# A two-layer transformer prompt kernel: the first tiles' statistics, the last output and the instruction order rearranged

## The chip, the core and the metric

The kernel runs on one core of a Trainium2 chip. The metric is the device time of one execution in microseconds. TensorE multiplies matrices (PE in the profile, PEld its weight loads), VectorE (DVE) and ScalarE (ACT) do elementwise work, GpSimd (POOL) a few masks at the start, and SyncE (SP) issues nearly all transfers between DRAM and on-chip memory. PSUM is the memory in eight banks into which TensorE accumulates.

## The reference

x is 2048 x 1024 in bf16. Two layers are computed with the same weights, each an attention part and a feed-forward part, both behind a layer norm and with a residual:

```
x = x + A(layernorm(x))      # qkv = x @ wqkv; 32 heads of 32; each position attends
                             # to 8 positions: itself and every second one before it; @ wo
x = x + B(layernorm(x))      # relu(x @ w1 + b1)**2 @ w2 + b2, inner width 3584
x = x + A(layernorm(x))
x = x + B(layernorm(x))
```

## The kernel before, in words

The 2048 rows are four blocks of 512 per layer, eight units u in all; a block is four tiles (tl) of 128 rows. A unit goes through: load and normalise x (SA), transpose it so that TensorE can contract over the width, the q, k and v products (SQ in eight-block form, SQ7 in a form with seven products of half blocks that needs sums and differences of weights), windowed attention (S2), the wo product and second layer norm (SW, SW7), and the two feed-forward products (SF1, SF2). The combined weights are made once in the first blocks and kept in DRAM tensors (sk, sqv, sw, two, tw); later blocks read them back. tw1 is one of the four combinations of w2, read in two halves by SF2.

Nothing is issued directly. Every step is an operation of a Plan with an engine, an assumed duration, a priority and the cells that it reads and writes. `Plan.schedule` plays the operations with these durations and takes on each engine the ready one with the lowest priority number; `emit` does so once per list in `ORDER`. The seeds of the first list move some priorities up or down by a hashed amount (`shift`), those of the later lists do so around the start times of the schedule before (`reshift`). The order thus found is the order in which the instructions stand on each engine; each engine executes its own in that order and waits by semaphores. SP too works through its transfers in that order, and a transfer also waits until the one that used the same of eight semaphores before it has landed. So new seeds move instructions everywhere.

The opening (SA for u = 0). Tiles are taken in the order `ORD` = 0, 1, 3, 2. `load_x` (the issue is recorded at L418, inside `dma`) loads a tile by SP, or by ScalarE for the tiles in `XACT`. Tiles 0 and 1 go through `ln_first`: two statistics of 512 columns on VectorE (L787), their aggregate (L789), logarithm and exponential on ScalarE (L780, L781), the normalisation on VectorE (L784), and then `transpose`: eight 128 x 128 transposes on TensorE (L803) into one PSUM bank and copies out of it (L806), in two parts of 512 columns. Tiles 2 and 3 (`LNA`) go through `ln`: sums and squares on ScalarE (L742, L746) and the normalisation on VectorE (L755, tile 3) or ScalarE (L721, tile 2), with one copy by ScalarE out of PSUM. `first` and `after` add dependencies: tile 1's statistics come after tile 0's last statistic, and tile 0's normalisation after tile 1's aggregate. Before all this TensorE runs 15 products of ones, and four more after tile 1's transposes (`keep_clock`, L1493). The first real products are those of q and k (SQ, L882), for the columns of tiles 0 and 1 first; their first chunk is in two parts, the first of which needs only the first part of the copies.

The transposes of later blocks are made by transfers (L768, `DMA_TRANSPOSE`) instead of TensorE.

The end (SF2 of the last unit, `out_tile`). The product T4 accumulates into the banks X[0] and X[1]. X[1] is the last, and its last seven contraction steps are split into two halves of 256 columns. `out_tile` with `end` adds each half of the bank to the residual xm on VectorE (L1450) and stores it; all other outputs go by a cast on ScalarE (L1051) and an addition on VectorE (L1052).

## Time and profile before

| | us |
|---|---|
| median of three runs | 1133.62 |
| lowest and highest | 1131.38, 1135.53 |
| the profiled execution | 1133.11 |
| its span in the profile | 1131.4 |
| TensorE busy | 1119.1 |
| VectorE busy | 991.6 |
| ScalarE busy | 814.4 |

The page counts an engine as busy while one of its instructions runs; matmuls overlap one another, and their ends are modelled. A row of the timeline merges equal neighbours: start, length from the first start to the last end, engine, line, operation, tiles, shape, count, and in brackets the idle time before with what ended it. A row of the issues gives the tensor, the queue, the count, the size of one transfer and the median time from issue to landing. A row of the waits gives who waited for whom: total, times, longest.

### The profile page before, as it was taken

Reading aid. Unit: us, or ns where it says so; the run is one execution under the profiler, and the core shown is the slowest. Engines: PE = TensorE matmul, PEld = TensorE weight load, DVE = VectorE, ACT = ScalarE, POOL = GpSimd, SP = SyncE. Lnnn points to the kernel's source line nnn. Section 1 sums busy time; section 2 is a strip of 40 time slices with the busy share of each in tenths; the row PEclk is TensorE's granted clock in tenths of the full one; section 3 lists DMA queues with packets and bytes.
Section 4 is the critical chain, followed back from the end, with each engine's and each line's share of the span. In section 5 each row is a group of like instructions: output and inputs, shape, how many; then the busy total and the mean of one; then the engine's idle time right before and its main releaser. Section 6 shows DMA issues by size and latency. Waiting matters only on the chain.

```text
span 1131.4 us, 20642 instructions
## 1 busy us (share of the span) xinstructions
PE 1119.1 (99%) x7856; PEld 770.6 (68%) x7903; DVE 991.6 (88%) x1527; ACT 814.4 (72%) x1631; POOL 1.8 (0%) x8
## 2 busy tenths in 40 slices
PE   9999999999999999999999999999999999999998
PEld 6645764678746887468864788557884678845864
DVE  6999999999996999969999699997999799996341
ACT  7747996568975799556994669937798378933961
POOL 0000000000000000000000000000000000000000
PEclk9999999999999999999999999999999999999999
DMA  9956899999899988999879997899969999589881
GB/s 369 288 190 204 269 326 327 337 356 375 345 362 361 330 358 310 297 392 330 355 288 346 399 365 271 296 381 364 395 212 351 374 363 388 197 297 341 340 302 62
DMA packets 137022, 362.35 MB, mean 320 GB/s; under 512 B 67418, under 2 KB 68570, under 8 KB 116570
## 3 DMA queue, kind: packets, MB, share of 16 engines
q1 hardware_dynamic: 136634, 360.50, 90.9%
q8 instruction: 62, 1.02, 0.4%
q10 hardware_dynamic: 288, 0.52, 0.1%
q14 instruction: 38, 0.31, 0.1%
HBM read 314.84 MB, written 31.46 MB: 306 GB/s over the span
## 4 chain that ended last, share of the span: by engine, by line
PE 92%; ACT 5%; DMA 2%; issue 1%; DVE 0%; ACTq 0%; DVEq 0%; SPq 0%
PE X L659 26%; PE X L1382 15%; PE Z L659 13%; PE Z L1382 7%; PE Y L659 7%; PE pq L882 6%; PE py L481 4%; PE Y L1382 4%; PE py L1078 4%; PE X L1149 3%; PE Z L1149 2%; PE lg L959 1%; DMA w<-in_B_w_dram 1%; PE Y L1149 1%; DMA xt<-xs 1%; ACT r L1317 1%
## 5 line engine op out<-in xcount | busy, mean ns | idle before, releaser
L659 PEld LDWEIGHTS <-w 128*128 128x128 bf16 (+1 forms) x4904 | 479.6, 98 | 71.3 <-DMA w<-sw 1.2
L1382 PEld LDWEIGHTS <-r 128*128 128x128 f16 x1183 | 115.7, 98 | 136.5 <-issue 1.7
L1382 PE MATMUL X<-w,r 128*128 128x512 f16 (+2 forms) x784 | 176.1, 377 | 1.6 <-ACT yxa L1051 1.3
L944 DVE TENSOR_TENSOR P<-q,k 128x2048 f16<-128x2048 f16 x128 | 154.3, 1221 | 2.4 <-ACT q L622 0.9
L659 PE MATMUL X<-T,w 128*128 128x256 f16 x1224 | 154.2, 273 | 0.3 <-ACT u L1286 0.3
L1023 DVE TENSOR_TENSOR pr<-pb,v 128x4096 f16<-128x4096 f16 x64 | 146.2, 2293 | 0.5
L952 DVE TENSOR_TENSOR P<-P,P 128x2048 f16<-128x2048 f16 x110 | 133.3, 1215 | 0.1
L1317 ACT ACTIVATE r<-rr 128x1024 f16<-128x1024 f16 x110 | 124.2, 1147 | 0.2
L1030 DVE TENSOR_TENSOR pr<-pr 128x2048 f16<-128x2048 f16 (+1 forms) x128 | 117.7, 947 | 0.0
L659 PE MATMUL X<-TA,w 128*128 128x256 f16 x864 | 107.2, 273 | 0.1
L882 PE MATMUL pq<-xnA,w 128*128 128x256 f16 (+1 forms) x512 | 86.1, 326 | 0.2 <-ACT k L887 0.2
L592 ACT COPY Y<-X 128x512 f32<-128x512 f32 x115 | 70.3, 611 | 19.8 <-PE X L659 15.3
L1296 ACT CAST y<-Z 128x512 f16<-128x512 f32 x110 | 70.3, 655 | 7.3 <-PE Z L659 7.1
L882 PEld LDWEIGHTS <-w 128*128 128x128 bf16 x512 | 49.9, 98 | 32.6 <-issue 0.7
L1300 DVE TENSOR_TENSOR rr<-u,y 128x512 f16<-128x512 f16 x110 | 45.5, 419 | 25.2 <-ACT y L1296 16.6
L1323 ACT ACTIVATE rr<-Y,b1T 128x256 f16<-128x256 f32 x110 | 54.6, 536 | 4.9 <-PE Y L659 4.3
L659 PE MATMUL X<-xnB,w 128*128 128x256 f16 x440 | 56.1, 273 | 0.1
L659 PE MATMUL Y<-xnB,w 128*128 128x256 f16 x440 | 56.0, 273 | 0.0
L614 ACT CAST yq<-Z 128x512 f16<-128x512 f32 x72 | 41.5, 586 | 19.7 <-PE Z L659 19.7
L1323 ACT ACTIVATE rr<-X,b1T 128x256 f16<-128x256 f32 x110 | 55.6, 570 | 0.0
L1051 ACT CAST yxo<-X 128x512 f16<-128x512 f32 x27 | 15.4, 586 | 55.5 <-PE X L1382 55.5
L610 ACT CAST u<-X 128x512 f16<-128x512 f32 x72 | 41.5, 586 | 18.6 <-PE X L659 18.1
(166 smaller groups left out, 1684.6 us busy)
## 6 DMA issues: line engine op xcount, KB each, us to landing
w<-sw SPq DMA_DIRECT2D x49, 1024.0 KB, 9.1
w<-tw SPq DMA_DIRECT2D x56, 896.0 KB, 6.7
w<-in_B_w_dram SPq DMA_DIRECT2D x42, 896.0 KB, 5.3
w<-in_B_w_dram SPq DMA_DIRECT2D x35, 1024.0 KB, 9.8
w<-in_A_wqkv_dram SPq DMA_DIRECT2D x32, 1024.0 KB, 10.1
w<-sqv SPq DMA_DIRECT2D x24, 1024.0 KB, 10.5
w<-in_B_w_dram SPq DMA_DIRECT2D x28, 512.0 KB, 6.3
w<-sk SPq DMA_DIRECT2D x12, 1024.0 KB, 8.2
```

The source lines that it names most:

```text
L592: self.p.add("ACT", act(512), lambda: self.nc.scalar.copy(Y[:], X[:]), [(X, 0)], [(Y, 0)], UP, name="u")
L659: nc.tensor.matmul(bank[:, a, :], lw[:, k, a * 128:(a + 1) * 128], rhs(k), start=(start and k == 0 and a == 0), stop=(k == 3), skip_group_ ...
L882: nc.tensor.matmul(pq[:, t0 * HB:t1 * HB], w[:, c0 // 2 % 2, kd // 4, kd % 4, c0 % 2 * 128:c0 % 2 * 128 + 128], xnT[:, 2 * t0:2 * t1, kd, ...
L944: nc.vector.tensor_tensor(cur[:], q[:, c, None, hb * HB:(hb + 1) * HB].to_broadcast([128, W, HB]), _win_ap(k[:, c, :], HALO + hb * HB, HB) ...
L952: nc.vector.tensor_tensor(other[:], other[:], cur[:], ALU.add)
L1023: p.add("DVE", dve(4096), lambda pr=pr, ch=ch: nc.vector.tensor_tensor(pr[:], pb[:].unsqueeze(1).to_broadcast([128, 2, W, HB]), _win_ap2(v ...
L1030: nc.vector.tensor_tensor(dst, pr[:, :, 0:n, :], pr[:, :, n:2 * n, :], ALU.add)
L1149: nc.tensor.matmul(bank[q][:], left(j, q), right(j), start=start and j == 0, stop=j == h - 1, skip_group_check=True)
L1296: p.add("ACT", act(512), lambda: nc.scalar.copy(y[:], bank[:]), [(bank, 0)], [(y, 0)], 1.5, name="y")
L1317: p.add("ACT", 0.955, lambda: nc.scalar.activation(out=r2[:, f:f + 2, :].rearrange("p a t -> p (a t)"), in_=r[:].rearrange("p a m t -> p ( ...
L1323: p.add("ACT", 0.36, lambda a=a: nc.scalar.activation(out=r[:, a, 0, :], in_=bank[:, a, :], func=ACTF.Relu, bias=self.b1T[:, f + a:f + a + ...
L1382: nc.tensor.matmul(banks[q][:, lo:hi], left(jj, q), w[:, j, lo:hi], start=(start and jj == 0), stop=(jj == h - 1), skip_group_check=True)
```

## The change

Opening: all four tiles of x are loaded by SP, in the order 0, 1, 3, 2 (`XACT` empty). Tile 3 leaves `LNA` and goes through `ln_first`, so its statistics and normalisation are VectorE's, and its copy too; only tile 2's statistics stay on ScalarE. Tile 1's statistics now come after tile 0's aggregate (`AGF`) instead of its last statistic, and tile 3's after tile 1's normalisation (`FNO`) instead of its copy. Where a tile's copies are in two parts, the second part goes to ScalarE (`CPA`).

End (`TAIL`): before the last, split contraction steps TensorE adds the residual of the last tile into its bank by one product with the identity. The bank is then copied out by two plain copies, the first half by VectorE with a store on SP's queue, the second by ScalarE with a store on ScalarE's queue.

Order: new seeds, in two lists instead of three.

```diff
-XACT = (1, 2)
+XACT = ()
...
-LNA = (2, 3)
+LNA = (2,)
+LNP = -9e4
+LNV = (3,)
+AGF = True
+FNO = True
+CPA = (1,)
+TAIL = True
...
 ORDER = [   # 55, 18 and 19 seeds replaced by 52 and 23 others
...
-            p.add("DVE", 0.5, f4, [(x, 0), (sm, 0), (sm, 1)], [(xn, 0)], -2e5 + pr, after=after, name="bn4")
-            return self.transpose(xn, xnT, tl, -1e5 + pr, 2 if tl < 2 else 1), xn
+            no = p.add("DVE", 0.5, f4, [(x, 0), (sm, 0), (sm, 1)], [(xn, 0)], -2e5 + pr, after=after, name="bn4")
+            return self.transpose(xn, xnT, tl, -1e5 + pr, 2 if tl < 2 else 1), xn, no
...
-            def f6(i=i):
-                (nc.scalar.copy if act else nc.vector.tensor_copy)(xnT[:, tl, i * n:(i + 1) * n], pt[:, i * n:(i + 1) * n])
+            on_act = act or parts > 1 and i in CPA
+
+            def f6(i=i, on_act=on_act):
+                (nc.scalar.copy if on_act else nc.vector.tensor_copy)(xnT[:, tl, i * n:(i + 1) * n], pt[:, i * n:(i + 1) * n])
...
-                    first, rest0 = [bn], rest
+                    first, rest0 = [ag] if AGF else [bn], rest
...
-                    c, xn = rest()
-                    first = [c]
+                    c, xn, no = rest()
+                    first = [no if FNO else c]
...
+                    if split and half and q and TAIL:
+                        xr = xm[3]
+                        self.pe(1, lambda: nc.tensor.matmul(banks[1][:], self.ident[:], xr[:, 0:BLK], start=False, stop=False, skip_group_check=True),
+                                [(xr, 0)], [(banks[1], 0)], name="pp")
...
+        if end and TAIL:
+            for i in range(2):
+                a, c = slice(i * HB, (i + 1) * HB), slice(db * BLK + i * HB, db * BLK + (i + 1) * HB)
+                p.add("ACT" if i else "DVE", act(HB) if i else dve(HB, False), lambda a=a, c=c, i=i: (nc.scalar.copy if i else nc.vector.tensor_copy)(o()[:, c], py[:, a]),
+                      [(py, i)], [(xm, (db, i))], -100.0, name="xo")
+                self.dma(lambda c=c: dst[:, c], lambda c=c: o()[:, c], [(xm, (db, i))], [(cell, (db, i))], 0.07, prio=-10.0, eng="ACT" if i else "SP")
+            return
```

## The prediction

> **What bounds the kernel now.** I read the page first: span, engines, chain.

> ```profile
> span 1131.4 us, 20642 instructions
> PE 1119.1 (99%) x7856; PEld 770.6 (68%) x7903; DVE 991.6 (88%) x1527; ACT 814.4 (72%) x1631; POOL 1.8 (0%) x8
> q1 hardware_dynamic: 136634, 360.50, 90.9%
> PE 92%; ACT 5%; DMA 2%; issue 1%; DVE 0%; ACTq 0%; DVEq 0%; SPq 0%
> ```

> TensorE is busy for 99% of the span and holds 92% of the chain that ended last. The change leaves its matmuls as they are but for one more, so it can gain only where TensorE waits: before its first product, in the stalls between, and after its last product. The second reading is therefore the table of waits for TensorE alone.

> ```profile
> PE pt L803 <- DVE xn L784: 1.6, 1, 1.6
> PE X L1382 <- ACT yxa L1051: 1.3, 1, 1.3
> ...
> PE Z L659 <- ACT rr L1323: 0.9, 1, 0.9
> PE X L659 <- ACT u L1286: 0.3, 1, 0.3
> PE pq L882 <- ACT k L887: 0.2, 1, 0.2
> ```

> The first row is the opening. The other four come to 2.7 us in over a thousand. So little is left to win in the body that a new order is more likely to add waits than to remove many. The DMA engines, 90.9% occupied, are the resource by which it could: a load placed a little later lands later still.

> The sum is made on the profiled execution (1133.11 us: span 1131.4 and 1.7 outside it). It gives a difference, which I add to the median of the three runs, 1133.62, half a microsecond above the profiled one. A measurement of this kernel can tell about 0.3% from no change: 3.4 us, so 1130.2 and 1137.0 are the borders.

> **The opening.** Third reading: the timeline of the first 17 us, with the issues of the loads and their time to landing.

> ```profile
> 0.80 0.87 SPq L418 DMA_DIRECT2D x<-in_A_x_dram  x2
> 0.80 0.90 ACTq L418 DMA_DIRECT2D x<-in_A_x_dram  x2
> 4.30:6.50 2.20, 2.15 (x8) 0.69 (x6) 1.83 (x3) 0.00 (x0) 0.00 (x0) 1.00 1.02 394
> 4.28 1.29 DVE L787 BATCH_NORM_STATS2 st<-x 128x6 f32<-128x512 bf16 x2 [2.73 <-DMA x<-in_A_x_dram]
> 5.94 0.69 DVE L787 BATCH_NORM_STATS2 st<-x 128x6 f32<-128x512 bf16 x1 [0.37 <-DMA x<-in_A_x_dram]
> 7.33 0.21 DVE L789 BATCH_NORM_AGGREGATE sm<-st 128x2 f32<-128x12 f32 x1
> 8.14 0.55 DVE L784 TENSOR_SCALAR xn<-x,sm 128x1024 f16<-128x1024 bf16 x1 [0.19 <-ACT sm L781]
> 8.67 1.49 DVE L806 COPY xnA<-pt 128x512 f16<-128x512 f16 x4
> 10.07 5.40 PE L882 MATMUL pq<-xnA,w 128*128 128x256 f16 x48
> 15.75 1.04 PE L882 MATMUL pq<-xnA,w 128*128 128x256 f16 x8
> 8.01 1.04 ACT L742 ACTIVATE xn<-x 128x1024 f16<-128x1024 bf16 x1
> 14.51 1.25 ACT L721 ACTIVATE xn<-x,sm 128x1024 f16<-128x1024 bf16 x1
> 3.26 0.48 SPq L418 DMA_DIRECT2D w<-in_A_wqkv_dram  x1
> w<-in_A_wqkv_dram SPq DMA_DIRECT2D x1, 512.0 KB, 8.2
> 1125.70 0.58 ACT L1051 CAST yxo<-X 128x512 f16<-128x512 f32 x1 [3.95 <-PE X L1382]
> ```

> Before, SP issues the tiles 0 and 3 of x and ScalarE the tiles 2 and 1, in that order, so tile 0 (used at 4.28) shares the DMA engines with tile 2, and VectorE waits until 5.94 for tile 1. After, SP issues all four, in the order 0, 1, 3, 2. A tile is 0.262 MB, at 394 GB/s 0.67 us. If those 0.67 us of tile 2's bytes no longer lie in front, tile 0 lands at 3.6, and tile 1 0.67 later, before it is needed; if the gain is nil, at 4.28. [...]

> VectorE then does tile 0's two statistics (1.29), its aggregate (0.1 to 0.2 beside the next), tile 1's two (1.29): 6.3. From the last aggregate to the end of tile 1's normalisation it took 7.33 to 8.69, that is 1.36, so this ends at 7.7, against 8.69 before. Here the order of the changed program takes something back: the first copy of tile 0 (0.42) is followed on VectorE by tile 3's two statistics (1.29), which have moved there from ScalarE, and only then by tile 1's first copy (0.42). That ends at 7.7 + 0.4 + 1.3 + 0.4 = 9.8. ScalarE's two half copies (I take 0.58 each, its copy of 512 columns) run from 8.1, after VectorE's first, to 9.3 and are covered by those statistics. The first product waits for the copy at 9.8 instead of starting at 10.07: −0.3. With tile 0 landing at 4.28 it would be 10.45: +0.4.

> What is late next is the weights: the fourth piece, issued at 3.26, lands 8.2 later, at 11.5. It is wanted after 16 products of 0.109 ((5.40 − 1.04)/40), at 9.8 + 1.75 = 11.55, so it just fits. Then tile 2: before, ScalarE finished tiles 2 and 3 from 8.01 to 15.76; after, it has one tile, but starts at about 10.6, behind tile 3's root, and needs some 6 us with three casts between. TensorE asks for it after 56 products and one set of transposes, at 16.5. The two fit to within a few tenths; up to 0.4 is the bound. Opening: −0.2, between −0.3 and +0.8.

> At the copies the split promises two engines at once, and the order shows otherwise: ScalarE's copy of tile 0 waits for VectorE's, and VectorE's of tile 1 for ScalarE's. No row of before shows two engines reading one bank. [...]

> **The end.**

> ```profile
> 1127.23 0.42 DVE L1450 TENSOR_TENSOR xm<-X,xm 128x256 bf16<-128x256 f32 x1 [5.02 <-PE X L1382]
> 1127.57 0.41 DVE L1052 TENSOR_TENSOR xm<-yxo,xm 128x512 bf16<-128x512 f16 x1
> 1127.90 0.42 DVE L1450 TENSOR_TENSOR xm<-X,xm 128x256 bf16<-128x256 f32 x1
> 1127.68 1.28 SPq L418 DMA_DIRECT2D out_dram<-xm  x3
> out_dram<-xm SPq DMA_DIRECT2D x1, 64.0 KB, 1.7
> x<-in_A_x_dram SPq DMA_DIRECT2D x1, 256.0 KB, 3.5
> x<-in_A_x_dram ACTq DMA_DIRECT2D x1, 256.0 KB, 4.7
> ```

> Three VectorE steps end at 1128.32 and SP's third store goes out at about 1128.6. After, one matmul adds the residual (0.22 on TensorE, its price below), VectorE copies one half (0.42, as the add), and ScalarE, which waits for that, the other (I take 0.4, less than its 0.58 for 512 columns), ready at 1128.05; its store leaves on its own queue. The middle step and its store keep their place, leaving at 1128.1. So the last store is issued 0.5 sooner and the end comes 0.4 sooner, less the 0.22: −0.2. ScalarE's queue has stood idle since the start, or, after the change, has never been used; at the start its load took 4.7 against SP's 3.5. If the store pays that 1.2 as well, the end is 0.4 to 0.9 later. I take −0.2, between −0.4 and +0.9, nearer to SP's row, since the gap at the start has the shared engines in it.

> **The new order.** The seeds are new, so every instruction may stand elsewhere. Three places differ enough to be costed.

> ```profile
> 468.19 1.06 ACT L742 ACTIVATE xn<-xt 128x1024 f16<-128x1024 bf16 x1 [3.26 <-DMA xt<-xs]
> 47.84 5.27 SPq L768 DMA_TRANSPOSE xnA<-xn  x1
> xnA<-xn SPq DMA_TRANSPOSE x1, 9.6
> 57.63 3.62 PE L882 MATMUL pq<-xnA,w 128*128 128x512 f16 x16
> 577.91 0.32 SPq L418 DMA_DIRECT2D w<-tw  x1
> w<-tw SPq DMA_DIRECT2D x1, 896.0 KB, 6.6
> w<-tw SPq DMA_DIRECT2D x1, 896.0 KB, 8.8
> 580.10 4.70 PE L1382 MATMUL X<-w,r 128*128 128x512 bf16 x21
> 586.14 1.67 PE L1382 MATMUL X<-w,r 128*128 128x512 f16 x7
> ```

> A 512-column product costs (4.70 − 1.67)/14 = 0.216 us.

> First, the 1.3 us wait at L1382: ScalarE stood in its statistics for a late load of x (idle 3.26 before 468.19), with the copy that TensorE wanted queued behind. In the new order 42 products lie between the release of that load and the statistics, 28 before, 3 us more. I take the wait as gone: −1.3, at most 0 if another comes in its place.

> Second, the last transposition for the second block: issued at 47.84, landed 9.6 later at 57.4, and the first product that needs it starts at 57.63, 0.2 to spare. In the new order the products between ScalarE's last cast ahead of that tile's normalisation and the first use fall from 57 to 45, 2.6 us. One 0.67 us load less lies ahead in SP's queue. If the landing follows ScalarE, TensorE waits 2.6 − 0.2 − 0.7 = 1.7. If it follows the bytes in the queue, it comes 0.7 sooner, and the first use 1.1 sooner (a set of logits, four products, has moved behind it, and the opening gives 0.2): 1.1 − 0.2 − 0.7 = 0.2. I take +1.0, between 0.2 and 1.7.

> Third, the second half of the combination tw1 in the second feed-forward stage. At 577.91 it took 6.6, to 584.5, and was used at 586.14: 1.6 to spare, with 35 wide products between release and use. In two of the later blocks the new order leaves 28 (61 and 73 products of both widths became 37): 1.5 less, so it still fits at 6.6. At 8.8, the slowest of these loads, each is 2.1 late. I take 0.5 for both, between 0 and 4.2.

> Sum: −0.2 − 0.2 − 1.3 + 1.0 + 0.5 = −0.2, so 1133.4.

> **The rivals.** Slower: late loads. The new order lets loads go out later against their use, with the engines 90.9% occupied. For it: spare times of 0.2 and 1.6 us above; against it: before shows no wait of TensorE for a weight. It decides from a landing of 6.7 us for tw1's half. At 8.8, and the transposition at 1.7: −0.2 − 0.2 − 1.3 + 1.7 + 4.2 = +4.2, 1137.8.

> Faster: the four waits of the body were accidents of the old order, and the new one has none: −2.7, opening −0.3, end −0.4: 1130.2, at the border itself. For it: each wait occurs once only. Against it: the tighter places just named.

> No use of the opening: tile 0 lands as before, tile 1's copy waits for tile 3's statistics, tile 2 is late, so that the change does not bring the first product forward at all: +0.8 in place of −0.2, the rest as forecast: 1134.4.

> **How the numbers follow.** Forecast 0.35, no use of the opening 0.20, late loads 0.30, no waits 0.15. The first two lie within 0.3%: 0.55; slower 0.30; faster 0.15. The predicted time is the likeliest's, 1133.4; its own range is 1131.5 to 1135.5 (the bounds of opening, end and transposition). The range for 8 in 10 reaches from near the fast case to the slow one, 1130.5 to 1138.0.

> **What would show it.** In the profile of the changed kernel: VectorE's first statistics at 3.6 and its tile-1 statistics without a wait; a copy of tile 1 behind tile 3's statistics, and the first product at 9.8; the first product of the second block waiting up to 1.7 us for the transposition; no wait of 1.3 near 470; TensorE waiting or not for w from tw1 near 450 and 857; ScalarE's last store landing within 1.7 us. I am wrong if a wait of TensorE over 1 us stands elsewhere, or if first product or end moved by over 1 us.

## The result and the profile after

The changed kernel took 1137.1 us (median of 22 runs, 1134.93 to 1142.31), the kernel before 1134.0 (22 runs, 1131.38 to 1136.14): a ratio of 1.0027, 95% interval 1.0018 to 1.0036. It is 3.1 us slower, where I had written 0.2 us faster. That lies inside the 0.3% that I had called about the limit of what can be told, but with 22 runs the interval excludes no change.

The profiled execution of the changed kernel was the slowest of the 22 (1142.31 us), so its waits are not typical ones; a second profile is shown below. First the page, then the waits of TensorE (total us, times, longest).

```profile
span 1140.6 us, 20659 instructions
PE 1121.8 (98%) x7857; PEld 771.2 (68%) x7904; DVE 995.5 (87%) x1528; ACT 814.0 (71%) x1628; POOL 1.8 (0%) x8
PE 64%; ACT 12%; DMA 7%; DVE 2%; issue 1%; SPq 0%; ACTq 0%; DVEq 0%
```

```profile
PE Z L663 <- DMA w<-sw: 2.7, 1, 2.7
PE Z L663 <- DVE T L699: 1.9, 1, 1.9
PE py L1084 <- DMA w<-in_A_wo_dram: 1.4, 1, 1.4
...
PE X L1388 <- ACT yxa L1057: 1.0, 1, 1.0
PE pq L888 <- DMA w<-in_A_wqkv_dram: 0.9, 1, 0.9
PE pq L888 <- ACT q L893: 0.9, 1, 0.9
```

Before, TensorE waited 2.7 us in four places behind the opening. Here it waits 8.9 us in six places of 0.9 and more, the first of them still in the opening, and none of them is one of the three that I had costed for the new order: the fourth weight piece (12.5), a copy of q (38.9), the second half of wo (224.5), the combination T (267.5), a piece of sw (280.0), a copy yxa (748.7).

The opening, in the timeline:

```profile
3.61 1.29 DVE L791 BATCH_NORM_STATS2 st<-x 128x6 f32<-128x512 bf16 x2 [2.06 <-DMA x<-in_A_x_dram]
8.00 1.28 DVE L791 BATCH_NORM_STATS2 st<-x 128x6 f32<-128x512 bf16 x2
8.12 1.07 ACT L812 COPY xnA<-pt 128x512 f16<-128x512 f16 x2 [1.02 <-DVE xnA L812]
9.22 0.42 DVE L812 COPY xnA<-pt 128x512 f16<-128x512 f16 x1
4.19 0.78 SPq L422 DMA_DIRECT2D w<-in_A_wqkv_dram  x1
9.70 1.91 PE L888 MATMUL pq<-xnA,w 128*128 128x256 f16 x16 [0.48 <-DVE xnA L812]
12.54 1.05 PE L888 MATMUL pq<-xnA,w 128*128 128x256 f16 x8 [0.94 <-DMA w<-in_A_wqkv_dram]
```

Up to the first product this is what I had written, to a tenth. Then the fourth piece of the weights, issued at 4.19 and not at 3.26, lands 8.3 later, at 12.49, and the seventeenth product waits 0.94 for it. The end:

```profile
1133.34 3.20 PE L1388 MATMUL X<-w,r 128*128 128x512 f16 x21
1136.58 0.43 DVE L1460 CAST xm<-X 128x256 bf16<-128x256 f32 x1 [5.23 <-PE X L1388]
1137.04 0.37 ACT L1460 CAST xm<-X 128x256 bf16<-128x256 f32 x1 [1.40 <-DVE xm L1460]
1137.45 0.39 ACTq L422 DMA_DIRECT2D out_dram<-xm  x1
```

From the start of the last product (1136.27; before, 1126.92) to the end of the span it is 4.30 us, 4.45 before; the added product takes 0.22 of that back.

### The profile page after: what moved, and what is told of

Its sections match the earlier page's. It is cut to its first block, busy times and chain, and to the rows that moved or that the text cites. A ratio compares the mean times of both kernels' runs of the same rounds, so it can differ in the third digit from the quotient of the medians.

```text
span 1140.6 us, 20659 instructions
## 1 busy us (share of the span) xinstructions
PE 1121.8 (98%) x7857; PEld 771.2 (68%) x7904; DVE 995.5 (87%) x1528; ACT 814.0 (71%) x1628; POOL 1.8 (0%) x8
## 3 DMA queue, kind: packets, MB, share of 16 engines
q8 instruction: 62, 1.02, 0.4%
## 4 chain that ended last, share of the span: by engine, by line
PE 64%; ACT 12%; DMA 7%; DVE 2%; issue 1%; SPq 0%; ACTq 0%; DVEq 0%
PE X L663 20%; PE X L1388 12%; PE Z L663 10%; PE Z L1388 6%; PE Y L663 5%; PE X L1155 3%; ACT r L1323 3%; PE Y L1388 3%; ACT rr L1329 2%; PE py L1084 2%; PE Z L1155 1%; DMA w<-in_A_wo_dram 1%; DMA w<-sw 1%; DMA xt<-xs 1%; ACT u L1292 1%
## 5 line engine op out<-in xcount | busy, mean ns | idle before, releaser
L663 PEld LDWEIGHTS <-w 128*128 128x128 f16 (+1 forms) x4904 | 480.4, 98 | 75.9 <-DMA w<-sw 3.0
L950 DVE TENSOR_TENSOR P<-q,k 128x2048 f16<-128x2048 f16 x128 | 154.5, 1225 | 2.2 <-ACT q L626 2.0
L1323 ACT ACTIVATE r<-rr 128x1024 f16<-128x1024 f16 x110 | 123.9, 1139 | 0.3
L663 PE MATMUL Z<-T,w 128*128 128x256 f16 x392 | 51.0, 274 | 4.6 <-DMA w<-sw 2.7
## 6 DMA issues: line engine op xcount, KB each, us to landing
w<-tw SPq DMA_DIRECT2D x56, 896.0 KB, 6.6
w<-in_B_w_dram SPq DMA_DIRECT2D x42, 896.0 KB, 6.2
w<-in_B_w_dram SPq DMA_DIRECT2D x28, 512.0 KB, 5.7
```

Of the source, the lines that this page charges most:

```text
L663: nc.tensor.matmul(bank[:, a, :], lw[:, k, a * 128:(a + 1) * 128], rhs(k), start=(start and k == 0 and a == 0), stop=(k == 3), skip_group_ ...
L950: nc.vector.tensor_tensor(cur[:], q[:, c, None, hb * HB:(hb + 1) * HB].to_broadcast([128, W, HB]), _win_ap(k[:, c, :], HALO + hb * HB, HB) ...
L1323: p.add("ACT", 0.955, lambda: nc.scalar.activation(out=r2[:, f:f + 2, :].rearrange("p a t -> p (a t)"), in_=r[:].rearrange("p a m t -> p ( ...
```

## The experiments

In most kernels below each engine is given its operations in a stored order, so that a part of one order can be put beside a part of the other, or one operation moved, and nothing else:

```diff
-                i = next((i for i, item in enumerate(ready[e]) if fits(item[2])), None)
+                i = 0 if ready[e] and ready[e][0][0] == turn.get(e, 0) and fits(ready[e][0][2]) else None
...
-        for i, seeds in enumerate(ORDER or [[]]):
...
+        for r, o in sorted(zip(ranks, self.ops), key=lambda x: x[0]):
+            o.prio = float(turn.setdefault(o.eng, 0))
+            turn[o.eng] += 1
+        order, self.timed = self.schedule()
```

`ranks` is the stored list; the first change makes `schedule` take only the operation whose turn it is on its engine.

**Opening and end against order.** e1 has the code of the changed kernel and its order for the first 18 us of the plan and in the end, the old order between. e2 is the reverse. e4 and e8 are the two kernels once more.

> Opening and end as in the changed kernel, every other operation in the order of the kernel before. Theory A (the new order of the body costs the 3 us: loads that go out later against their use): only the opening and the end are left, +0.7 and -0.1 by the two profiles, so 0.6 us over the kernel before, a ratio of 1.0005, and none of the waits of TensorE near 39, 224, 267, 280 that the profile of the changed kernel has. Theory B (the opening costs them: all weights land 1.1 us later and everything behind runs late): 3 us over before, 1.0027, with new waits in the first 60 us. In both, the wait of 0.9 us for a piece of the weights behind the sixteenth product stays.

> The reverse: opening and end as before, every other operation in the order of the changed kernel. Theory A: 2 to 3 us over before, a ratio of 1.0018 to 1.0027, with waits of TensorE of 0.9 to 2.7 us at the places of the changed kernel (about 0.7 us earlier). Theory B: within 0.5 us of before, 1.000. If both this kernel and the one with the old order stay below 1.001, the two parts cost only together.

> The changed kernel once more, beside the others: 1.0027 of before, and a second profile. Theory A in its plain form: the waits of over 1 us (224, 267, 280, 748) stand in it again, with the same length, since they follow from the order. If they are accidents of one execution, only those of the opening (0.9 for the weight) and at 39 come back. A stretch of half clock behind the wait at 280 should come back with the wait, and not without it.

> The kernel before once more, for a second profile: which of its waits return. The wait of 1.3 for yxa near 470 and that of 0.9 near 262 should, by the view that an order fixes its waits; the one of 1.6 in the opening must.

e1 took 1.0000 of before (0.9991 to 1.0008), e4 1.0028 (1.0016 to 1.0040). So the opening and the end cost nothing that can be told, and the order of the body costs the 3 us: theory B is out. e2 took 1.0069 (1.0056 to 1.0082), 7.8 us, far more than either theory had. The timeline of VectorE shows why: the operation b2d in e2, in the changed kernel and in the kernel before (e8). The last line is what TensorE then waited for in e2, at 32.2:

```profile
30.18 0.69 DVE L1479 TENSOR_TENSOR b2d<-b2b 128x512 f32<-128x512 bf16 x1 [5.67 <-DMA b2b<-in_B_b_dram]
```

```profile
25.41 0.69 DVE L1496 TENSOR_TENSOR b2d<-b2b 128x512 f32<-128x512 bf16 x1 [1.29 <-DMA b2b<-in_B_b_dram]
```

```profile
30.09 0.69 DVE L1479 TENSOR_TENSOR b2d<-b2b 128x512 f32<-128x512 bf16 x1
```

```profile
PE lg L959 <- DVE P L952: 4.1, 1, 4.1
```

In the new order b2d stands ahead of five operations on P for which TensorE waits later. With the new opening b2b lands at 25.4 and VectorE loses 1.29 us; with the old one it lands some 5 us later and VectorE loses 5.67. In the old order b2d stands five operations further back and nothing waits.

The second profile of the changed kernel (e4), waits of TensorE from 20 us on:

```profile
PE Z L663 <- DMA w<-sw: 1.7, 1, 1.7
PE X L1388 <- ACT yxa L1057: 1.2, 2, 1.0
PE py L1084 <- DMA w<-in_A_wo_dram: 0.5, 1, 0.5
PE Z L1388 <- ACT yxa L1057: 0.3, 1, 0.3
```

The waits for sw, wo and yxa come back; those for q near 39 and for T near 267 do not. Of the old order's four, the second profile (e8) has three (0.2, 1.0 for yxa, 0.3) and not the 0.9 near 262, but 3.0 in two waits for pieces of w1 that the first did not have. So single waits between 220 and 290 vary by up to 2 us from one execution to the next, in both kernels, and one profile of each could not have settled the matter.

To sum up such profiles I use TensorE's lag: the start of a product less the time of all products ahead of it at 0.2157, 0.1092 and 0.0558 us (512, 256 and 128 columns), worked out from the starts in each trace and counted from the first product of q and k; products whose records a trace lacks are counted too. What a row gains from column to column is what TensorE lost there.

```
at (us of products)    20    160    215    285    330    720    760    end
before               10.4   10.6   10.7   12.0   12.0   13.8   13.9   14.3
before again (e8)    10.3   10.5   10.5   13.9   13.9   15.2   15.2   15.7
e1                   10.6   10.8   10.8   13.2   13.2   14.4   14.4   14.9
changed              10.8   12.1   13.7   20.4   21.0   21.3   22.6   23.1
changed again (e4)   10.6   10.8   11.5   13.4   14.0   14.5   16.1   16.3
e9  (old, less DMA)  10.5   10.7   10.7   10.7   10.8   11.6   11.6   12.1
e10 (new, less DMA)  11.0   11.9   12.9   12.9   13.6   13.8   13.8   14.4
e16 (new, b2d back)  11.2   11.5   11.6   13.8   14.3   14.4   15.6   16.2
e18 (old, b2d ahead) 10.5   12.9   12.9   17.6   17.6   19.0   19.0   19.5
```

**The weights in the order of their use.** A buffer is made for each piece in the order k, q, k, q, so that the queue can follow it:

```diff
+        for nm in jobs + jobs if pieces else ():
+            ws[nm].append(Buf("8K", "w", [128, 2, 2, 4, 256], BF))
```

> The changed kernel, but its first eight pieces of wqkv go out in the order in which TensorE uses them (k, q, k, q), so that the piece for the seventeenth product is second in the queue and not fourth. Theory A: the wait of 0.94 us goes (the piece lands near 9.9, wanted at 11.6), the opening gives 0.2 to 0.4 us against before instead of costing 0.7, and the total falls by 0.9 us to about 2.2 over before, 1.0019. Theory B: the total falls by more than 2 us, to 1.001 or less, since what follows runs on time again. If the wait only moves to the next pieces, 1.0027 stays.

> Opening and end of the changed kernel, the order of before elsewhere, and the first eight weight pieces in the order of their use. The kernel without that last step took the time of before (1.000). If the opening is worth what its own times say, first products 0.4 sooner and no wait for the seventeenth product: 0.4 to 1.0 us below before, 0.9991 to 0.9996. If a later wait swallows it (at 30 or at 57, where the next block's first products wait for ScalarE or the transpositions), 1.000.

Neither is faster. The wait of 0.94 went in both. But e3 took 1.0032 (1.0021 to 1.0044), and in its profile TensorE waits 2.12 at 39.8 for ScalarE; e11 took 1.0016 (1.0007 to 1.0024), slower than e1, and waits 0.41 at 18.1 for a later piece of the same weights and 0.87 at 31.4 for a copy of k. What the fourth piece gains, other waits take back: in e11 the one for a later piece is shown, what makes q late in e3 is not.

**Which third of the order.** New order up to 152 us of the plan, from 152 to 329, or from 329 on, the old order elsewhere; opening and end as changed.

> Opening and end as in the changed kernel; the new order only up to 152 us of the plan (the first block's attention and feed-forward and the making of the combinations that are stored), the old order behind it. It stands against the kernel with the old order throughout, which took the time of before (1.000). Theory C (a debt: in the new order the first stores of combinations go out at 94.8 instead of 91.4, the DMA engines stand idle longer between 80 and 95, and by 220 us some 0.7 MB less has moved than in the old order, 2 us at 0.36 MB per us, which the loads between 220 and 290 then pay): +1.5 to +2.5 us, a ratio of 1.0013 to 1.0022, with waits of TensorE for wo near 222 and for w from sw near 275, though the order there is the old one. Theory D (the order in which loads, transpositions and stores are issued between 152 and 329 costs by itself): 1.000, none of these waits. A wait of TensorE near 39, if ScalarE is late there, belongs to both.

> The reverse: old order up to 152 us of the plan, new order from 152 to 329, old order from there. Theory D: +2 us or more, 1.0018 or above, waits for wo near 222 (0.5 to 1.5) and for w from sw near 275 (1.7 to 2.7), and the two of 0.3 near 310 and 314. Theory C: at most the two of 0.3, 1.0005 or less, and the waits near 222 and 275 are gone or under 0.5.

> Old order up to 329 us of the plan, new order behind it. Both theories: what the profiles of the changed kernel show there (a wait of 1.0 near 745 for a copy that stands behind ScalarE's statistics, 0.3 to 0.5 at two more places) against what the old order has there (0.7 to 1.3 near 470, 0.4 near 984): within 0.8 us, 1.000 to 1.0007. More than 1.0015 would say that the loss is spread over the later blocks and that neither theory has it.

1.0022 (1.0010 to 1.0033), 1.0017 (1.0008 to 1.0026), 1.0013 (1.0004 to 1.0022). Every third costs, 2.5, 1.9 and 1.5 us, together more than the whole. Neither theory C nor D holds: the loss is not in one stretch. Part of the surplus may be the seams: TensorE waits 1.0 at 154.5 in e5 and 0.4 at 334.8 in e7, where the two orders meet, and in no profile of either kernel.

**Less for the DMA engines to move.** The two kernels in their own orders:

```diff
-            self.dma(lambda: self.scr["w1"][dp][:, i], src, r, ...
+            self.dma(lambda: self.scr["w1"][dp][0:8, i], lambda: src()[0:8], r, ...
-    ... lambda d=d: self.scr[job][d][:], ...
+    ... lambda d=d: (self.scr["k"]["k", 0] if job == "w1" else self.scr[job][d])[:], ...
     (the same for two, read from tw)
```

> The kernel before, in its own order, with less to move: the stores of w1's and wo's combinations (sw and two, 36 of them, 0.26 MB each) write 8 of 128 partitions, and what is loaded from them later is taken from another scratch of the same size, so that the results of the later blocks are not those of the reference. Some 9 MB fewer pass the DMA engines between 100 and 270 us. It is the base for the next kernel. Theory E (late loads behind a full queue are what the waits of TensorE between 220 and 290 are made of, in both orders): its waits near 254, 262 and 271 go, 1 to 3 us less than before, 0.9975 to 0.999. Theory F (the waits come from the order in which ScalarE and VectorE do their work): no change, 1.000.

> The changed kernel in its own order with the same stores cut down. Theory E: the waits near 222, 267 and 275 to 280 go with the backlog, 2.5 to 5 us less than the changed kernel, and the distance to the kernel before with the same cut falls from 3.1 us to 1 or less (the opening and the waits of 0.3 to 1.0 near 310 and 742 stay). Theory F: the distance stays near 3.

The waits of e9 and those of e10, all that are over 0.2 us (left out is only the one of 1.1 before the first products of ones, which every profile has):

```profile
PE pt L803 <- DVE xn L784: 0.7, 1, 0.7
PE X L1382 <- ACT yxa L1051: 0.4, 1, 0.4
PE X L659 <- ACT u L1286: 0.3, 1, 0.3
```

```profile
PE pq L888 <- DMA w<-in_A_wqkv_dram: 1.1, 1, 1.1
...
PE py L1084 <- DMA w<-in_A_wo_dram: 0.8, 1, 0.8
PE pq L888 <- DVE xnA L812: 0.7, 1, 0.7
PE pq L888 <- ACT q L893: 0.5, 1, 0.5
PE Z L1388 <- ACT yxa L1057: 0.3, 1, 0.3
PE X L663 <- ACT u L1296: 0.3, 1, 0.3
```

The first half of theory E holds: without 9 MB of stores no load is waited for between 225 and 290 in either kernel, and both get faster, to 0.9973 (0.9964 to 0.9983) and 0.9997 (0.9987 to 1.0006) of before. The second half does not: the distance is still 0.0024, or 2.7 us (2.5 by the medians, 1133.73 and 1131.25, of runs that spread from 1130.73 to 1132.14 in e9 and from 1131.36 to 1136.58 in e10), and the wait for wo near 224, which theory E had counted in, stays at 0.8. Late loads behind a full queue (DMA share 1.05 from 220 to 290 in the kernel before, 1.06 in the changed one) are what both orders wait for there; they are not the difference between the two. In the lag table e10 is behind e9 by 0.5 us at 20, 1.2 at 160, 2.2 at 215 (wo), 2.8 at 330 and 2.3 at the end: in these two profiles nearly all of the distance has arisen by 215.

**Moving forward what TensorE waits for.** e13 moves nine operations of the changed kernel, e14 a tenth, e15 four of the kernel before:

```diff
 e13  SP       wo, first half     ahead of 4 stores of tw   (206.99)
               wo, second half    ahead of 3 stores of tw   (214.10)
      ScalarE  u, u, Y<-X         ahead of r, rr            (308, 313)
               yxa x4             ahead of xn statistics    (739, 742)
 e14  + SP     w<-sw              ahead of 2 stores of two  (260)
 e15  SP       w<-in_B_w, twice   ahead of 2 stores of two  (244, 259)
      ScalarE  yxa                ahead of xn statistics    (471)
               u                  ahead of y                (985)
```

> The changed kernel with nine operations moved forward on their own engine's queue and nothing else: both halves of wo ahead of the four and the three stores of tw in front of them; three operations of ScalarE near 308 and 312 (u, u, the copy Y<-X) ahead of activations that nobody waits for yet; four casts yxa near 738 and 740 ahead of a tile's statistics. Theory G (the distance is made of the waits that recur in every trace of the new order, 0.7 to 1.6 for wo, 0.6 near 310 to 314, 1.3 to 1.6 near 740): these go, 2.4 to 3.2 us less than the changed kernel, 0.9995 to 1.0005 of before. Theory H (they only cover others: what is late behind them shows up next, at 225 to 290 and at 875): less than 1 us, 1.0018 or more.

> As e13, and the piece of sw that TensorE waits for near 275 to 280 (0 to 2.7 us, once with a stretch of half clock behind it) goes out ahead of the two stores in front of it, 0.5 MB or 1.4 us sooner. Theory G: 0.5 to 1.5 us less than e13, if the engines are as far behind there as in the traces so far, 0.9985 to 1.000. If the wait moves to the next load, the same as e13.

> The kernel before, with four operations moved forward: two pieces of w1 ahead of the two stores in front of each (waits of 1.7 to 1.9 near 254 and 1.0 to 1.5 near 271, in most traces of the old order), one cast yxa near 470 ahead of a tile's statistics (0.5 to 1.4), and one cast u near 984 (0.4). Theory G says the same here: 1.4 + 1.0 + 0.9 + 0.4, less what the moved loads cannot make up: 2 to 3.5 us less than before, 0.997 to 0.998, and so faster than either kernel. Theory H: within 0.5 us of before.

e13 took 1.0044 (1.0029 to 1.0059) and e14 1.0061 (1.0048 to 1.0074): slower than the changed kernel. The wait for wo, in e13:

```profile
PE py L1084 <- DMA w<-in_A_wo_dram: 2.4, 1, 2.4
```

Its first half, four places further forward, went out at 207.96, where e4 sent it at 206.99, and the stores behind it with it. VectorE's idle time between 200 and 220, by the starts and ends in the trace, rose from 0.3 (e4) to 2.7 us. The load seems to need a buffer that VectorE still reads, and VectorE the buffers of the stores; that is argued, not shown. Only yxa near 740 was repaired as listed. In the old order the four moves paid: e15 took 0.9988 (0.9979 to 0.9997), 1.4 us less than before where 2 to 3.5 were expected, the fastest version of the study that does the whole work. All four waits are gone from its profile, and a new one of 2.3 us for sw has come.

**VectorE.** The share of the page (DVE 87 or 88%) hides a stretch in which it is full. The last line of a table of stretches from 20 to 240 us (220 us), of before and of the changed kernel:

```profile
sum 220.00, PE 219.32 PEld 136.32 DVE 219.18 ACT 160.91 POOL 0.00; mean PE 43.86 PEld 27.26 DVE 43.84 ACT 32.18 POOL 0.00
```

```profile
sum 220.00, PE 217.25 PEld 135.87 DVE 215.19 ACT 158.75 POOL 0.00; mean PE 43.45 PEld 27.17 DVE 43.04 ACT 31.75 POOL 0.00
```

VectorE is idle for 0.8 us there in the old order, 4.8 in the new (2.9 in e4), and TensorE, busy for 219.32 in the old order, has no slack either. So e16 moves b2d back where the old order has it, e17 adds ScalarE's moves of e13 (with the second copy Y<-X), and e18 moves b2d two places forward in the old order.

```diff
 e16, e17   VectorE, from 22.7:  P<-P,P  -b2d  P<-P,P  P<-q,k x3  P<-P,P  +b2d
 e18        VectorE, from 25.8:  P<-q,k x2  +b2d  P<-q,k  P<-P,P  -b2d
```

> The changed kernel with one operation of VectorE moved: b2d (0.69 us), which waits 1.36 us for the load of b2b near 24, goes behind five operations on P, where the old order has it. Theory V (VectorE is the engine that is full between 20 and 260, and its idle time is carried forward to the buffers of wo and to the combinations T, so that a microsecond lost there is lost once more on TensorE): VectorE's idle time between 20 and 40 is gone, wo's wait near 222 falls from 0.7 to 1.6 to 0.5 or less, 1.0 to 1.5 us less than the changed kernel, 1.0012 to 1.0020 of before. Rival W (the idle time is absorbed by later waits of VectorE, at 160 to 180 for the store of sqv): no change, 1.0025 or more.

> As e16, and on ScalarE: u, u and two copies Y<-X near 308 to 314 ahead of activations that nobody waits for, four casts yxa near 738 to 740 ahead of a tile's statistics. Theory V with the recurring waits: 1.2 for wo, 0.6 near 310, 1.4 near 740, in all 2.5 to 3.2 us less than the changed kernel: 0.9995 to 1.0006 of before. Rival W: only the last two, 1.0010 to 1.0015. More than 1.002 would say that the waits only change places.

> The kernel before with b2d moved forward by two operations on VectorE, so that VectorE waits some 1.8 us for b2b (landing near 29.5) in the old order too. Theory V: TensorE's waits near 30 (0.3), at 222 (none so far) and between 254 and 272 grow by 1 to 2 us in all, 1.0009 to 1.0018. Rival W: within 0.5 us of before, 1.000.

VectorE's wait in e18, from its timeline:

```profile
30.01 0.69 DVE L1479 TENSOR_TENSOR b2d<-b2b 128x512 f32<-128x512 bf16 x1 [1.86 <-DMA b2b<-in_B_b_dram]
```

That one move, two places on an engine that is not the page's bound, cost 1.0025 (1.0015 to 1.0035), 2.8 us. In the lag table 2.4 are lost by 160, where both profiles of the kernel before lose 0.2, and another 4.7 between 215 and 285 (a wait of 2.9 for a piece of w1, with a stretch of half clock behind it), where they lose 1.3 and 3.4. With e2 it shows that idle time of VectorE in this stretch is paid by TensorE. The way back does not show as much: e16 took 1.0023 (1.0014 to 1.0032). Its waits for VectorE's hole and for wo are gone (0.1 left at 222), but VectorE has 1.1 us of idle time between 40 and 100, where the changed kernel has 0.8 in its first profile and none in e4, and the 0.5 us less than the changed kernel is within both intervals. e17 took the same, 1.0023 (1.0014 to 1.0033), with the wait near 740 gone, wo's back at 1.2, and 2.3 for sw.

**Idle time and the clock.** In the changed kernel's profiled execution 16 products from 281.19 on, behind the wait of 2.74 that ends at 280.0, took 3.26 us; 16 such products take 1.91 elsewhere. The table of stretches gives the granted clock behind the busy times (0.57 for 280 to 284).

```profile
280.00:284.00 4.00, 4.00 (x22) 2.94 (x23) 2.21 (x2) 1.76 (x4) 0.00 (x0) 0.57 1.02 416
```

> None of the kernel's work: TensorE does groups of 56 products of 512 columns (12 us), and between two groups waits for VectorE's copies of 128 to 4096 columns out of PSUM, so that it stands idle for some 0.3 to 5 us, in rising steps, twice over. It tells at what idle time the products that follow run at half clock, and for how long. From the traces so far: no stretch of half clock after waits of up to 1.93 us, one of some 3.4 us after waits of 2.28, 2.74 and 4.1. If idle time alone decides, the border lies between 1.93 and 2.28 in both passes; if not (the time since the last such stretch, or what TensorE did before), the two passes differ, or waits of 2.5 here pass at full clock.

Three groups of 56 products from its timeline, one of each kind:

```profile
152.49 12.25 PE L57 MATMUL pk<-ones 128*128 128x512 f16 x56 [2.10 <-DVE t L60]
166.97 13.93 PE L57 MATMUL pk<-ones 128*128 128x512 f16 x56 [2.23 <-DVE t L60]
200.09 12.25 PE L57 MATMUL pk<-ones 128*128 128x512 f16 x56 [2.69 <-DVE t L60]
```

Behind the first group, up to 1.97 us of idle time every group ran at full clock; from 2.82 on every one had a slow stretch, which in most costs 1.7 us (13.93 − 12.25). Between, 2.10 and 2.23 were slow in one pass and fast in the other, 2.56 slow in both and 2.69 fast in both, so the length of the wait alone does not decide there.

Where the wait falls does. In the trace's record of the granted clock the 18 slow stretches of e12 all begin at whole multiples of 3.4133 us from one another, to 0.01 us; the one in the changed kernel's trace begins 276.48 us behind the start of the record, 81 times 3.4133, and lasts 3.413. Cut into windows on that grid, TensorE's time looks like this: a window around a wait and the one behind it, for waits of 2.10 (first pass), 2.10 (second pass) and 2.69 (second pass). The second number of a row is TensorE's busy time, the third from the end the granted clock.

```profile
150.64:154.05 3.41, 1.56 (x8) 0.72 (x8) 1.73 (x3) 0.00 (x0) 1.00 0.00 0
154.05:157.46 3.41, 3.41 (x18) 1.52 (x17) 0.00 (x0) 0.00 (x0) 1.00 0.00 0
471.49:474.90 3.41, 1.31 (x7) 0.58 (x6) 1.94 (x3) 0.00 (x0) 1.00 0.00 0
474.90:478.32 3.42, 3.42 (x10) 1.22 (x8) 0.00 (x0) 0.00 (x0) 0.50 0.00 0
519.27:522.68 3.41, 1.39 (x7) 0.67 (x7) 1.87 (x4) 0.00 (x0) 1.00 0.00 0
522.68:526.10 3.42, 3.42 (x18) 1.54 (x17) 0.00 (x0) 0.00 (x0) 1.00 0.00 0
```

Idle are 1.85, 2.10 and 2.02 us of these windows, and only the second is followed by half clock. The same holds for every window of the 20 traces in which TensorE ran at full clock, from 14 us to the last product (the grid of each placed by the stretch of half clock that its record has behind the last product): with 2.02 us or less of idle time in one window no half clock followed, with 2.10 or more it always did. The wait of 2.35 for wo in e13 passed at full clock; the grid cut it, with 1.87 in the longer part.

## Why the prediction was wrong, step by step

The step that failed is the term for the new order. The sum has it at +0.2 (−1.3 + 1.0 + 0.5); e4 against e1, which differ in the order of the body alone, puts it at 3.2 us (1.0028 against 1.0000). The other terms were off by less than a microsecond and are taken first.

Opening, first product: right. That tile 0 would land at 3.6 and not at 4.28 was a choice, which no run had shown: in the first 6 us of before SP's queue holds 45.9% of the engines' time and ScalarE's 23.3%. With SP's queue alone tile 0's statistics began at 3.61, the first product at 9.70 (9.8), through tile 3's statistics as described. What failed here is the fourth weight piece, "issued at 3.26, lands 8.2 later, at 11.5 … it just fits". I took its issue from the kernel before, though I had just moved two loads in front of it on the same queue: it went out at 4.19, 0.93 later. The 17th product came 0.7 later instead of 0.2 sooner (at 12.54; before, without a wait, at 10.07 + 16 x 0.109 = 11.81), inside my bounds; by the column for 20 us of the lag table 0.2 to 0.4 of it is left. In e1, with the old order behind it, nothing of this was left in the total.

End: right within 0.3 (−0.2 written; −0.15 and +0.22 measured). ScalarE's store took 1.9 to land, SP's of the same size 1.6: not the 1.2 more that I had allowed for.

The 1.3 us at L1382 ("I take the wait as gone"): gone near 470, but the same thing stands near 740, a cast yxa behind the statistics of a tile: 1.0 us in both profiles. The upper bound ("at most 0 if another comes in its place") was nearly the right value.

The last transposition (+1.0) and the halves of tw1 (+0.5): both nothing. The transposition was issued at 53.12, landed in 5.0 at 58.12, and its product began at 58.25, with 0.1 to spare (in e17, with the same order there, it waited 0.3); near 450 and 857 no wait of over 0.1.

So of the three places priced one was near its bound and two came to nothing, and the loss is elsewhere. My own sign of being wrong, a wait of over 1 us in another place, came true three times (wo, T, sw). The fault lies in the costing itself: I looked for places at which a load comes nearer to its product, and priced three. The order also moves VectorE's operations, and I read VectorE as 88% busy. In the stretch from 20 to 240 it is at 219.18 of 220 us. I never asked what each reordered operation of VectorE waits for; b2d is one row of its timeline. VectorE thus stood in the sum at nothing, with no reason given.

The rival "late loads" had 1137.8, near the measured 1137.1, by luck: its two terms, the transposition and tw1, came to nothing, and e10 refutes its reason as the cause of the distance. The forecast's own range was also added up wrongly: the bounds that it names give 1132.3 to 1136.2, not 1131.5 to 1135.5, and the measured time lies above both. What the runs settle: the order, not the opening or the end; spread over all thirds; not the full queue; a hole in VectorE's work can do it (e2, e18). What stays open is which part of the 3.1 us is b2d's, wo's, sw's or yxa's: taking out one of them (e16, e17) gave back at most half a microsecond, and others came in its place.

## What to carry to other kernels

Read the busy share by stretches before trusting the share of the span: an engine that is full for 220 us is a bound there (VectorE here, 219.18 of 220; a wait of 1.86 on it cost 2.8 in e18), and each operation that a new order moves on it has to be asked what it waits for. Where loads are moved to a queue, look at every later issue on that queue: here the fourth weight piece went out 0.93 later, at 4.19 instead of 3.26, behind two loads more. And where a kernel's waits differ by 2 us from one execution to the next, take two profiles of each before a wait is repaired; most of the repairs here that moved a waited-for operation forward only moved the wait.
